# One table for the order and the engines of an attention and gated-MLP kernel on one core

## Chip, core and metric

The kernel runs on 1 core of one Trainium2 chip, in one launch. The metric is the device time of one execution in microseconds (us). The median of three runs of the kernel before is 904.5 us (904.38 to 905.22).

## What is computed

The reference, cut to what matters. `q`, `k` and `v` are 4 x 8 x 768 x 64 (batch, head, position, dimension) in float32, `proj` is 64 x 6, the three weights are 512 x 1536, 512 x 1536 and 1536 x 512:

```python
q_bucket = sum((q @ proj > 0) * 2 ** arange(6))     # hash of each position, the same for k
scores = where(q_bucket[..., :, None] == k_bucket[..., None, :], q @ k.T / 8, -1e9)
attn = exp(scores - max(scores));  attn = attn / (sum(attn) + 1e-09)
x = (attn @ v).transpose(0, 2, 1, 3).reshape(3072, 512)
out = ((x @ w_a) * (x @ w_b)) @ w_out
```

## The kernel before

**Work.** The 3072 tokens are cut into 14 chunks of one or two times 128 tokens (`BLOCKS`). For each chunk the attention output is computed first and then sent through the gated MLP. The last matmuls of a chunk stand in the program between those of the attention of later chunks.

**Attention.** `kprep` and `qprep` (L1127 on) load k and q and call `split` (L709), which scales a tensor by a power of two, writes it as a float16 high part (`kt0`, `qt0`, L648 or L646) and a low part (L748), copies the high part (`hp`, L639), turns both by 128x128 transposes (L766 on PE, with the copy `trk` or `trq` at L639, or by DMA at L757), and adds the hash bits as 12 further rows (L787, L805 to L817). `vprep` (L1031) loads v and makes `vh` and `vl` (L1051). For each tile of 128 queries, `qtile` (L1202) has: scores on PE (L1215), the maximum on DVE (`mx`, L1235), two small steps that give scale and bias (`sc`, `bias`, L1243 and L1247, on DVE or POOL), the exponential on ACT (`e`, L1256). In chunk 0 `turned` (L1181) transposes `e` on PE (`et`, L1191) and copies it back (`at`, L639). In all other chunks `by_dma` (L1163) casts it to a high part `a` (L639, on ACT, DVE or POOL), subtracts that for a low part (L642, on POOL), and turns both by DMA (L1177). Then PE multiplies by v (`av`, L1269 or L1284). After 8 tiles (a chunk of 128 tokens, or half of a larger one) `su_end` (L1292) divides by the sums (`x`, L1335) and turns the result (`px`, `xT`, L1376).

**Weights.** All three weights (18 blocks, two DMAs each) are loaded once, at the start. `to_f32` (L921) loads a block into one of three staging slots (L934, a ring: the fourth block's load waits until the first slot is free) and rebuilds exact float32 values with three steps: a low piece (`third`, L945 on ACT or L947 on POOL), a high piece (L955 on ACT), and both together on DVE (L963), which frees the slot. Every two blocks then get a bound from PE (`slot_gram`, L981, 16 matmuls), DVE (L662) and `power_of` (`w_ai`, L625 and L628).

**MLP.** `moe` (L1389): `ab` on PE (L1442 in float32 for the first two chunks, L1450 with three float16 products for the others), product of both halves on ACT, DVE and POOL (L1471 to L1495), `o` on PE (L1515), `osb` and the store.

**What sets the order.** The functions above only record operations, numbered as they are recorded; each has its engine or the engines allowed, an estimated duration, and what it reads and writes. `Plan.issue` (L400) then replays them with these durations as a list scheduler: whenever an engine is free in the replay, the ready operation with the lowest number in `PLACES` is issued on it (an engine that `ENGINES` names, or the first free one of several). The order in which operations are issued is the order of each engine's instructions, and every engine takes its instructions in that order: one that waits holds back all that stand behind it. The loads and DMA transposes are issued by SP, in its own order. Two recorded operations (`lambda: None`, for `identh` and `identb`) only mark tokens and issue nothing.

Of the kernel before, what the change touches and what calls it, by code (L numbers as in the profile page):

```python
# [61 lines left out]
PLACES = (  # L62
# [234 lines left out]
    3481: "DVE", 3489: "DVE", 3497: "DVE", 3505: "ACT", 3514: "ACT", 3522: "DVE", 3538: "DVE", 3547: "DVE",  # L297
    3568: "ACT", 3576: "ACT", 3584: "ACT", 3592: "DVE", 3601: "ACT", 3634: "DVE", 3635: "DVE", 3725: "DVE",
}

def free(b, **durs):
# [27 lines left out]
HOP = 0.2  # L331
PE_TAIL = 0.2
# [34 lines left out]
class Plan:  # L367
# [32 lines left out]
    def issue(self):  # L400
        ops = self.ops
        for o, place in zip(ops, PLACES):
            o.key = place
            o.eng = ENGINES.get(o.seq, o.eng)
# [1214 lines left out]
```

## Time and profile before

| | us |
|---|---|
| median of three runs | 904.5 |
| lowest and highest run | 904.38, 905.22 |
| span of the profiled execution, first to last instruction | 900.4 |
| busy: PE, DVE, ACT, POOL | 871.8, 624.4, 573.4, 450.9 |

The profile gives the profiled execution by its span; a time of its own, measured as the runs are, is not shown, so 904.5 - 900.4 = 4.1 us are taken as what lies around the span. Lines (L963) are those of the kernel before. A busy time on PE runs from a matmul's start to its modelled end and the matmuls overlap, so that the length of a short row holds some 0.1 to 0.2 us of the row behind it; on DVE and ACT a step's end overlaps the next start by about 0.1 us.

### The profile page before, as it was taken

What the parts mean: (1) busy time and instruction counts of PE and PEld (TensorE: products, weight loads), DVE (VectorE), ACT (ScalarE), POOL (GpSimd) and SP (SyncE); (2) the same over time, 40 slices, a digit from 0 to 9 for tenths busy, and PEclk for the clock granted to TensorE, in tenths of its full rate; (3) what the DMA queues carried; (4) which work ended last, traced back from release to release, by engine and by line L of the source; (5) the groups of instructions that cost most, each with busy time, mean ns of one, the idle gap of its engine ahead of it and who ended that gap; (6) DMA issues with size and microseconds to landing.
All of it is one profiled execution on the core that took longest, in us unless ns stands there. A gap on an engine that the chain in (4) does not pass through costs nothing.

```text
span 900.4 us, 24310 instructions
## 1 busy us (share of the span) xinstructions
PE 871.8 (97%) x9761; PEld 673.8 (75%) x9761; DVE 624.4 (69%) x1446; ACT 573.4 (64%) x1125; POOL 450.9 (50%) x377
## 2 busy tenths in 40 slices
PE   5798999999999999999999999999999999999998
PEld 4677788786877777777777777777777777777775
DVE  6889878897778666777776686777778576633211
ACT  5986565677776878666766675667676466654222
POOL 1255456555735665554455556635556457544111
PEclk9699999999999999999999999999999999999999
DMA  9898667599998999998976788698986757755100
GB/s 331 262 319 232 124 112 158 124 179 220 190 230 148 170 163 161 177 209 169 176 161 128 149 175 169 115 214 170 179 183 148 124 136 130 147 95 100 32 24 24
DMA packets 430433, 145.31 MB, mean 161 GB/s; under 512 B 404080, under 2 KB 422640, under 8 KB 430320
## 3 DMA queue, kind: packets, MB, share of 16 engines
q1 hardware_dynamic: 430160, 143.76, 76.8%
q8 instruction: 76, 1.25, 0.6%
q14 instruction: 37, 0.30, 0.1%
q10 hardware_dynamic: 160, 0.00, 0.0%
HBM read 37.82 MB, written 6.29 MB: 49 GB/s over the span
## 4 chain that ended last, share of the span: by engine, by line
PE 85%; DVE 9%; DMA 2%; issue 2%; ACT 1%; POOL 0%; SPq 0%; DVEq 0%; ACTq 0%; POOLq 0%
PE ab L1450 37%; PE o L1515 20%; PE s L1215 12%; PE av L1284 10%; PE ab L1442 4%; DVE mx L1235 2%; DVE wz L963 1%; PE kt L766 1%; DMA wz<-in_moe_w_out_dram 1%; DVE wz L906 1%; DMA wz<-in_moe_w_b_dram 1%; DMA wz<-in_moe_w_a_dram 1%; DMA pj<-in_proj_dram 0%; PE qb L787 0%; DVE g L1479 0%
## 5 line engine op out<-in xcount | busy, mean ns | idle before, releaser
L642 POOL TENSOR_TENSOR a<-e,a 128x768 f16<-128x768 f32 x184 | 309.4, 1686 | 199.3 <-DVE a L639 87.9
L1450 PE MATMUL ab<-xT,wz 128*128 128x256 f16 (+1 forms) x3456 | 377.5, 264 | 1.4 <-DVE g L1479 1.0
L1450 PEld LDWEIGHTS <-wz 128*128 128x128 f16 x3456 | 310.9, 98 | 52.5 <-issue 3.5
L1256 ACT ACTIVATE e<-s,bias,sc 128x768 f32<-128x768 f32 x192 | 189.8, 989 | 107.4 <-DVE bias L1247 84.5
L1235 DVE TENSOR_REDUCE mx<-s 128x1 f32<-128x768 f32 x192 | 182.7, 953 | 64.1 <-PE s L1215 59.0
L1515 PE MATMUL o<-wz,g 128*128 128x512 f16 (+1 forms) x840 | 215.6, 392 | 0.1
L1495 POOL TENSOR_TENSOR g<-g,g 128x256 f16<-128x256 f32 x132 | 95.8, 726 | 170.8 <-ACT g L1490 164.3
L1215 PE MATMUL s<-trk,trq 76*128 76x384 f16 (+1 forms) x768 | 157.6, 330 | 3.8 <-ACT e L1256 2.5
L1479 DVE SCALAR_TENSOR_TENSOR g<-ab,ab,a 128x256 f32<-128x256 f32 x132 | 63.4, 480 | 105.6 <-ACT a L1471 88.0
L1284 PEld LDWEIGHTS <-at 128*128 128x128 f16 x3312 | 116.9, 98 | 16.2 <-issue 1.7
L1515 PEld LDWEIGHTS <-g 128*128 128x128 f16 x792 | 73.8, 98 | 68.8
L1471 ACT ACTIVATE a<-ab,ab 128x256 f32<-128x256 f32 x132 | 62.2, 471 | 96.2 <-PE ab L1450 79.8
L1284 PE MATMUL av<-vh,at 128*128 128x64 f16 x2208 | 121.6, 193 | 0.7 <-DMA at<-a 0.7
L1215 PEld LDWEIGHTS <-trq 76*128 76x128 f16 (+1 forms) x768 | 70.7, 99 | 45.7 <-issue 9.5
L639 ACT CAST a<-e 128x768 f16<-128x768 f32 x105 | 87.0, 829 | 3.4 <-DMA at<-a 1.4
L1490 ACT CAST g<-g 128x256 f16<-128x256 f32 x132 | 53.0, 401 | 51.3 <-DVE g L1479 41.1
L1284 PE MATMUL av<-vl,at 128*128 128x64 f16 x1104 | 62.3, 193 | 0.0
L639 DVE CAST a<-e 128x768 f16<-128x768 f32 x71 | 42.2, 596 | 14.6 <-ACT e L1256 13.7
L1442 PE MATMUL ab<-xT,wz 128*128 128x128 f32 x384 | 48.1, 278 | 1.3 <-DVE xT L639 0.8
L1442 PEld LDWEIGHTS ab<-xT,wz 128*128 128x128 f32 x384 | 45.5, 192 | 4.6 <-DVE xT L639 1.5
L1247 DVE TENSOR_SCALAR bias<-mx,sc 128x1 f32<-128x1 f32 x180 | 38.6, 214 | 6.3
L1243 DVE TENSOR_SCALAR sc<-mx,cq 128x1 f32<-128x1 f32 x180 | 38.1, 212 | 4.8
(170 smaller groups left out, 775.4 us busy)
## 6 DMA issues: line engine op xcount, KB each, us to landing
rk<-in_k_dram SPq DMA_DIRECT2D x16, 384.0 KB, 4.2
rq<-in_q_dram SPq DMA_DIRECT2D x24, 256.0 KB, 3.5
wz<-in_moe_w_a_dram SPq DMA_DIRECT2D x12, 512.0 KB, 5.7
wz<-in_moe_w_b_dram SPq DMA_DIRECT2D x12, 512.0 KB, 5.3
wz<-in_moe_w_out_dram SPq DMA_DIRECT2D x12, 512.0 KB, 5.7
out_dram<-osb SPq DMA_DIRECT2D x24, 256.0 KB, 2.5
vr<-in_v_dram SPq DMA_DIRECT2D x12, 384.0 KB, 4.7
at<-a SPq DMA_TRANSPOSE x184, 3.5
```

Source lines behind the costliest of these rows:

```text
L639: {"ACT": nc.scalar.copy, "DVE": nc.vector.tensor_copy, "POOL": nc.gpsimd.tensor_copy}[e](out=out, in_=x)
L642: (nc.gpsimd if e == "POOL" else nc.vector).tensor_tensor(out=out, in0=x, in1=y, op=ALU.subtract)
L1215: nc.tensor.matmul(ps.t[:, jj, :HALF], lhsT=trq.t[rows, i, (2 * j + h) * nt + t], rhs=tr.t[rows, i, k0 : k0 + NT // 2].rearrange("p n s -> ...
L1235: lambda: nc.vector.tensor_reduce(out=mx.t[:, col], in_=halves(ps.t), axis=AX.XY, op=ALU.max, negate=True),
L1256: lambda: nc.scalar.activation(flat2(e.t), halves(ps.t), AF.Exp, bias=bias.t[:, col], scale=sc.t[:, col], accum_out=sm.t[:, u : u + 1],),
L1284: nc.tensor.matmul(av.t[:, u, :], lhsT=at.t[:, a + kt, :], rhs=w.t[:, h, kt, :], start=i == 0, stop=i == 3 * NT - 1,)
L1442: nc.tensor.matmul(pl.t[:, m, to], lhsT=wt32(m, cc, f), rhs=xt.t[:, cc * nt // NC, cc * nt % NC : cc * nt % NC + nt, :], start=cc == 0, st ...
L1450: nc.tensor.matmul(pl.t[:, m, to], lhsT=wt(m, wi, cc, f), rhs=xt.t[:, cc * nt // NC, xi, cc * nt % NC : cc * nt % NC + nt, :], start=i == ...
L1471: lambda a=a, pl=pl, gr=gr, sc_of=sc_of: nc.scalar.activation(a.t, pl.t[:, 0, :CH], AF.Copy, scale=sc_of(gr)),
L1479: lambda a=a, g32=g32, pl=pl, gr=gr, sc_of=sc_of: nc.vector.scalar_tensor_tensor(out=g32.t, in0=pl.t[:, 1, :CH], scalar=sc_of(gr + 1), in1 ...
L1495: lambda g=g, g32=g32, g_of=g_of: nc.gpsimd.tensor_tensor(out=g_of(g[1]), in0=g32.t, in1=g_of(g[0]), op=ALU.subtract),
L1515: nc.tensor.matmul(po[u].t.rearrange("p a b -> p (a b)"), lhsT=x()[:, us], rhs=w, start=f == 0 and i == 0, stop=f == NF - 1 and i == len(t ...
```

## The change

`PLACES`, `ENGINES` and the list scheduler go. `ORDER` gives the numbers of all operations in the order in which they are issued, and `ENGINE_OF` one engine for each operation that may run on several. `issue` walks through the list and checks that predecessors are issued and that buffers do not run out. The two operations that issue nothing are dropped and their tokens go to the operations that write the constants, so numbers shift by one or two. What every operation does is as before.

```diff
-PLACES = (
-    372, 36, 26, 591, 571, 25, 386, 254, 1614, 66, 385, 210, 155, 399, 576, 261, 194, 687, 615, 294, 3076, 750, 536,
...
-ENGINES = {
-    17: "DVE", 20: "ACT", 27: "ACT", 33: "DVE", 36: "DVE", 43: "ACT", 49: "DVE", 52: "DVE", 53: "ACT DVE",
...
+ORDER = (
+    9, 10, 75, 76, 4, 77, 11, 2, 0, 3, 78, 79, 80, 84, 12, 13, 14, 27, 28, 1, 5, 81, 15, 16, 82, 29, 281, 83, 6, 282,
...
+ENGINE_OF = {
+    "ACT": (
+        19, 26, 42, 51, 58, 67, 74, 80, 83, 84, 90, 105, 107, 109, 111, 121, 130, 138, 140, 147, 149, 157, 159, 166, 168,
...
     def issue(self):
-        ops = self.ops
-        for o, place in zip(ops, PLACES):
-            o.key = place
-            o.eng = ENGINES.get(o.seq, o.eng)
...
+        engine = {n: e for e, ns in ENGINE_OF.items() for n in ns}
+        issued, live = set(), {}
+        for n in ORDER:
+            o = self.ops[n]
+            assert o.preds <= issued, n
+            issued.add(n)
...
+            if isinstance(o.dur, dict):
+                o.fn(engine[n])
+            else:
+                o.fn()
...
-    op("DVE", 0.2, lambda: None, -85, r=["csb"], w=["identh"])
...
-        op("DVE", 0.2, lambda: None, key, r=["csb"], w=["identb"])
```

The order of PE's operations differs from the old one up to the 384th of 1056, which ran at 284.1 us in the trace before, and is the same behind it; on the other engines the last difference lies between 281 and 285 us too. Of the operations that may run on several engines, 127 get another one, all of them in that stretch. By kind: 9 low pieces of weight blocks go from ACT to POOL (one comes back); 17 pairs of `sc` and `bias` go from DVE to POOL and 6 the other way; 16 casts of `e` go from ACT or DVE to POOL and 3 from POOL to ACT; 14 subtractions for the low part of `e` go from POOL to DVE; 15 high parts and copies of them in `split` go from ACT to DVE and two the other way; 5 copies `at` of chunk 0 go from ACT to DVE and 3 the other way.

**DVE, the last instructions ahead of the first `x` (chunk 0's attention output).** In the names `wz` is the weight store, `po_t` and `ai` are powers of two, `mx_1_0` is the row maximum of chunk 1. Before:

```order
L639 COPY at_0_0_2_1_0_961<-et_0_0_2_1_0_0_969 128x384
L662 TENSOR_REDUCE wost_776<-gram_wo1_978 128x1
L662 TENSOR_REDUCE st_q2_0_1017<-gram_q2_0_997 128x1
L639 CAST a2_1_0_0_0_0_1019<-e_1_0_0_0_0_973 128x768
L963 SCALAR_TENSOR_TENSOR wz_70<-wz_70 128x1024
L625 TENSOR_SCALAR po_t_q2_0_1034<-ps_q2_0_1024 128x1
L628 SCALAR_TENSOR_TENSOR ai_q2_0_1035<-pw_74,po_t_q2_0_1034 128x2
L1226 TENSOR_SCALAR cq_2_0_1044<-ai_q2_0_1035,ai_k0_2_382 128x1
L1226 TENSOR_SCALAR cq_2_0_1044<-ai_q2_0_1035,ai_k0_0_148 128x1
L1226 TENSOR_SCALAR cq_2_0_1044<-ai_q2_0_1035,ai_k0_3_431 128x1
L1235 TENSOR_REDUCE mx_1_0_910<-s_1_0_2_1_0_1027 128x1
L1335 TENSOR_TENSOR x_0_0_1058<-av_0_0_615,r_0_0_930 128x512
```

Now, from five rows ahead of it to five rows behind it:

```order
L1156 TENSOR_REDUCE mx_1_0_886<-s_1_0_0_1_0_869 128x1
L583 TENSOR_REDUCE st_q4_1_899<-gram_q4_1_890 128x1
L884 SCALAR_TENSOR_TENSOR wz_70<-wz_70 128x1024
L1156 TENSOR_REDUCE mx_1_0_886<-s_1_0_0_0_0_914 128x1
L1246 RECIPROCAL r_0_0_852<-r_0_0_852 128x8
L1256 TENSOR_TENSOR x_0_0_929<-av_0_0_641,r_0_0_852 128x512
L546 TENSOR_SCALAR po_t_w0_934<-ps_w0_932 128x1
L549 SCALAR_TENSOR_TENSOR w_ai0_935<-pw_74,po_t_w0_934 128x2
L583 TENSOR_REDUCE wst_463<-gram_w2_944 128x1
L884 SCALAR_TENSOR_TENSOR wz_70<-wz_70 128x1024
L1156 TENSOR_REDUCE mx_1_0_886<-s_1_0_3_1_0_969 128x1
```

Of the 14 weight blocks whose last step (L963, now L884) stood ahead of `x_0_0`, five now stand behind it. So do three of the four `vl`, the four `w_ai` and three bounds. In all, 30 operations that stood ahead of `x_0_0` on DVE are behind it or on another engine, and 14 are new ahead of it: five copies `at`, three pairs of `sc` and `bias`, two high parts and two copies of them, the low part of one q, and one bound of q.

**POOL, its first instructions behind the constants.** L947 (now L868) is the low piece of a weight block; `hp` is the copy of a high part. Before:

```order
L639 COPY hp1_77<-qt0_0_0_193 128x8x64
L639 COPY hp0_76<-kt0_0_1_252 128x12x64
L947 ISA
L947 TENSOR_SCALAR wz_70<-wz_70 128x1024
L1243 TENSOR_SCALAR sc_0_0_480<-mx_0_0_424,cq_0_0_189 128x1
L1247 TENSOR_SCALAR bias_0_0_482<-mx_0_0_424,sc_0_0_480 128x1
L639 COPY hp0_76<-kt0_0_3_473 128x12x64
L947 TENSOR_SCALAR wz_70<-wz_70 128x1024
L1243 TENSOR_SCALAR sc_0_0_480<-mx_0_0_424,cq_0_0_189 128x1
```

Now:

```order
L868 ISA
L868 TENSOR_SCALAR wz_70<-wz_70 128x1024
L560 COPY hp1_77<-kt0_0_0_143 128x12x64
L868 TENSOR_SCALAR wz_70<-wz_70 128x1024
L560 COPY hp0_76<-kt0_0_1_171 128x12x64
L1164 TENSOR_SCALAR sc_0_0_365<-mx_0_0_363,cq_0_0_306 128x1
L1168 TENSOR_SCALAR bias_0_0_367<-mx_0_0_363,sc_0_0_365 128x1
L868 TENSOR_SCALAR wz_70<-wz_70 128x1024 x2
L560 COPY hp0_76<-kt0_0_3_402 128x12x64
L868 TENSOR_SCALAR wz_70<-wz_70 128x1024 x2
```

Of the first nine weight blocks, seven low pieces that ACT had are on POOL now, mixed with the copies and the small steps; the copy for `kt0_0_0` stands behind the first of them.

**SP, the first loads.** Before:

```order
L1017 DMA rk_0_0_93<-in_k_dram 128x2x384
L1144 DMA rq_0_0_95<-in_q_dram 128x8x64
L576 DMA ident_64<-in_cst_dram 128x128
L1017 DMA rk_0_1_100<-in_k_dram 128x2x384
L1065 DMA v0_2_102<-in_v_dram 128x2x384
L1065 DMA v0_0_110<-in_v_dram 128x2x384
L1065 DMA v0_3_126<-in_v_dram 128x2x384
L934 DMA wz_70<-in_moe_w_a_dram 128x1024
L1065 DMA v0_1_134<-in_v_dram 128x2x384
L934 DMA wz_70<-in_moe_w_a_dram 128x1024
```

Now, the first rows and those that follow them:

```order
L1065 DMA rq_0_0_84<-in_q_dram 128x8x64
L938 DMA rk_0_0_99<-in_k_dram 128x2x384
L498 DMA ident_64<-in_cst_dram 128x128
L938 DMA rk_0_1_126<-in_k_dram 128x2x384
L855 DMA wz_70<-in_moe_w_a_dram 128x1024 x2
L938 DMA rk_0_2_178<-in_k_dram 128x2x384
L855 DMA wz_70<-in_moe_w_a_dram 128x1024 x2
L938 DMA rk_0_3_219<-in_k_dram 128x2x384
L855 DMA wz_70<-in_moe_w_b_dram 128x1024 x2
L986 DMA v0_1_300<-in_v_dram 128x2x384
L986 DMA v0_3_303<-in_v_dram 128x2x384
L1065 DMA rq_1_0_326<-in_q_dram 128x8x64
```

```order
L855 DMA wz_70<-in_moe_w_b_dram 128x1024 x2
L986 DMA v0_2_370<-in_v_dram 128x2x384
L855 DMA wz_70<-in_moe_w_out_dram 128x1024 x2
L986 DMA v0_0_554<-in_v_dram 128x2x384
L855 DMA wz_70<-in_moe_w_out_dram 128x1024 x2
```

The q of the first chunk is loaded first, the four v (`v0_0` to `v0_3`) stand behind three, three, four and five weight blocks (in the order `v0_1`, `v0_3`, `v0_2`, `v0_0`), where they stood among the first nine loads; `v0_0` is behind the fifth block's loads, whose staging slot has to be freed first.

On PE, the first `ab` stands behind 80 operations instead of 85. Three of the seven `slot_gram` that stood ahead of it are behind it now, with three `power_of`, and one bound of a q (L675, four matmuls) is new ahead of it.

## Rows read from the trace of the kernel before

**Rows 1.** The page, its head and part 1 (busy time, share of the span, instructions).

```profile
span 900.4 us, 24310 instructions
...
PE 871.8 (97%) x9761; PEld 673.8 (75%) x9761; DVE 624.4 (69%) x1446; ACT 573.4 (64%) x1125; POOL 450.9 (50%) x377
```

**Rows 2.** Busy time by engine in five stretches (start:end, length, busy us and count).

```profile
0.00:76.50 76.50, 56.60 (x568) 47.96 (x568) 63.24 (x149) 60.33 (x86) 25.41 (x32) 0.87 0.93 293
76.50:100.00 23.50, 22.91 (x225) 19.40 (x226) 22.19 (x36) 15.71 (x25) 9.24 (x7) 1.00 0.67 182
100.00:200.00 100.00, 99.01 (x1212) 79.53 (x1211) 84.48 (x183) 63.52 (x116) 57.16 (x43) 1.00 0.71 145
200.00:300.00 100.00, 98.07 (x1268) 75.80 (x1267) 74.89 (x189) 72.70 (x152) 60.20 (x51) 1.00 0.99 194
300.00:900.40 600.40, 595.21 (x6494) 451.14 (x6492) 379.59 (x892) 361.17 (x750) 298.89 (x248) 1.00 0.74 141
```

**Rows 3.** Timeline of PE: start, length, line, output, what idle time ended on.

```profile
6.01 0.16 PE L613 MATMUL ps_pj<-st_pj,onesr 128*128 128x1 bf16 x1 [6.01 <-ACT pjx L653]
...
76.51 5.62 PE L1442 MATMUL ab<-xT,wz 128*128 128x128 f32 x48 [0.81 <-DVE xT L639]
82.25 1.08 PE L981 MATMUL gram_w<-wz 128*128 128x128 bf16 x16
```

**Rows 4.** Timeline of DVE before the first normalised output x.

```profile
66.47 1.82 DVE L963 SCALAR_TENSOR_TENSOR wz<-wz 128x1024 int32<-128x1024 int32 x1
...
69.72 1.23 DVE L963 SCALAR_TENSOR_TENSOR wz<-wz 128x1024 int32<-128x1024 int32 x1
...
73.74 0.68 DVE L1335 TENSOR_TENSOR x<-av,r 128x512 f32<-128x512 f32 x1
```

**Rows 5.** DVE groups by line and shape, 0 to 77 us (count, busy us, mean ns).

```profile
L963 DVE SCALAR_TENSOR_TENSOR wz<-wz 128x1024 int32<-128x1024 int32 x14 | 17.6, 1265 | 2.7 <-ACT wz L945 1.4 <-POOL wz L947 1.2
L1235 DVE TENSOR_REDUCE mx<-s 128x1 f32<-128x768 f32 x12 | 11.4, 948 | 2.2 <-PE s L1215 1.3 <-PE ps_k L613 0.8
...
L1051 DVE SCALAR_TENSOR_TENSOR vl<-v,v_ai,vh 128x768 f16<-128x768 f32 x4 | 4.1, 1013 | 0.0
L639 DVE COPY trk<-kt 128x1536 f16<-128x1536 f16 x3 | 2.8, 948 | 0.0
L1226 DVE TENSOR_SCALAR cq<-ai_q,ai_k 128x1 f32<-128x1 f32 x11 | 2.0, 208 | 0.1
...
L628 DVE SCALAR_TENSOR_TENSOR w_ai<-pw,po_t_w 128x2 int32<-128x2 f32 x4 | 1.6, 396 | 0.1
L639 DVE COPY at<-et 128x384 f32<-128x384 f32 x3 | 1.6, 543 | 0.0
...
L748 DVE SCALAR_TENSOR_TENSOR qt<-rq,ai_q,qt 128x512 f16<-128x512 f32 x2 | 1.9, 965 | 0.1
...
L648 DVE TENSOR_SCALAR vh<-v,v_ai 128x768 f16<-128x768 f32 x2 | 1.1, 610 | 0.0
...
L639 DVE CAST a<-e 128x768 f16<-128x768 f32 x1 | 0.5, 547 | 0.0
```

**Rows 6.** Chain that ended last, three pieces around 40 to 49 us (start, length).

```profile
40.76 4.70 DMA wz<-in_moe_w_a_dram
...
45.67 1.16 ACT wz L955
...
48.69 4.85 DMA wz<-in_moe_w_b_dram
```

**Rows 7.** POOL groups by line and shape, 0 to 77 us.

```profile
L947 POOL TENSOR_SCALAR wz<-wz 128x1024 int32<-128x1024 uint8 x7 | 8.9, 1267 | 22.8 <-DVE wst L662 9.0 <-DMA wz<-in_moe_w_b_dram 5.5 <-DMA wz<-in_moe_w_out_dram 2.2
```

**Rows 8.** Timeline of POOL around those two steps of DVE.

```profile
66.11 1.12 POOL L947 TENSOR_SCALAR wz<-wz 128x1024 int32<-128x1024 uint8 x1 [0.29 <-DMA wz<-in_moe_w_a_dram]
69.77 4.29 POOL L642 TENSOR_TENSOR a<-e,a 128x768 f16<-128x768 f32 x2 [2.54 <-DVE a L639]
```

**Rows 9.** POOL groups by line and shape, 76.5 to 300 us.

```profile
L642 POOL TENSOR_TENSOR a<-e,a 128x768 f16<-128x768 f32 x54 | 93.4, 1736 | 62.4 <-DVE a L639 36.1 <-ACT a L639 17.8 <-issue 2.9
```

More of the change, by code (lines that the diff above doesn't have):

```diff
@@ L1 @@
-import heapq
 from contextlib import ExitStack
@@ L299 @@
+ORDER = (
[187 rows of a table added]
+)
+ENGINE_OF = {
+    "ACT": (
[11 rows of a table added]
+    ),
+    "DVE": (
[17 rows of a table added]
+    ),
+    "POOL": (
[13 rows of a table added]
+    ),
 }
@@ L350, in __init__ @@
         self.shape, self.dtype, self.name = shape, dtype, name
-        self.real, self.left, self.free_at = None, 0, 0.0
+        self.real, self.left, self.held = None, 0, False
     @property
@@ L400, in issue @@
     def issue(self):
-        ops = self.ops
-        for o, place in zip(ops, PLACES):
-            o.key = place
-            o.eng = ENGINES.get(o.seq, o.eng)
-        for o in ops:
-            o.succs, o.npred, o.ready = [], len(o.preds), 0.0
-        for o in ops:
-            for p in o.preds:
-                ops[p].succs.append(o)
-        free = {e: 0.0 for e in ("PE", "ACT", "DVE", "POOL", "SP")}
-        ready = {e: [] for e in free}
-        for o in ops:
-            if not o.npred:
-                for e in o.eng.split():
-                    ready[e].append(o)
@@ L501, in issue @@
-        return now
+        engine = {n: e for e, ns in ENGINE_OF.items() for n in ns}
[4 more added lines that the diff above has]
+            issued.add(n)
+            for b in o.bufs:
+                if not b.held:
+                    b.held = True
+                    for k, limit in b.limits:
+                        live[k] = live.get(k, 0) + 1
+                        assert live[k] <= limit, (n, k)
+            if isinstance(o.dur, dict):
+                o.fn(engine[n])
+            else:
+                o.fn()
+            for b in o.bufs:
+                b.left -= 1
+                if not b.left:
+                    for k, _ in b.limits:
+                        live[k] -= 1
+                    if b.ring is not None:
+                        b.ring.append(b.real)
@@ L504, in attention_moe @@
+        assert len(issued) == len(self.ops)
 @with_exitstack
@@ L740, in high @@
                 nc.vector.tensor_copy(out=identh, in_=ident)
+        first = ["identh"] * (x == "0_0" and which == "k")
         op(
             "ACT DVE", {"ACT": 0.3 + 0.83e-3 * size, "DVE": 0.24 + 0.54e-3 * size},
-            high, key, r=[*toks, ai], w=[(pt[0], "hi")], sbuf=True,
+            high, key, r=[*toks, ai] + ["csb"] * len(first), w=[(pt[0], "hi"), *first], sbuf=True,
         )
@@ L865, in both @@
                 )
-        op("DVE", 0.2, both, key, r=[*((wst, g) for g in range(NG)), wo_ai], w=[wm], sbuf=True)
+        op("DVE", 0.2, both, key, r=["csb", *((wst, g) for g in range(NG)), wo_ai], w=[wm, "identb"], sbuf=True)
         ps = psum("ps_bounds", tag)
```

122 lines of the change are left out of this document (removed), and 417 rows, old and new, of tables (ENGINE_OF, ORDER, PLACES).

## Prediction

> **What bounds the kernel now.** I read the page's busy times first, then the same by stretch, then what PE waited for in the one stretch where it waits. PE is busy 871.8 of 900.4 us [rows 1]. By stretch [rows 2] the rest is uneven: behind 300 us PE is busy 595.21 of 600.40 us, and from 100 to 300 us 2.9 us are missing; in the first 76.5 us 19.9 are, and the mean granted clock there (the column behind the counts) is 0.87, which is 1.00 everywhere else. So the kernel is PE's own work, with a start in which PE waits. The timeline of PE shows the two ends of that start [rows 3]: the first matmul waits until 6.01 us for the projection, and the first `ab` of the MLP stands at 76.51 us, behind a copy on DVE. In between DVE is the full engine: busy 63.24 of the 76.5 us [rows 2], though it gets nothing from PE before 6.01 us, so nine tenths of the rest. From 76.5 us on PE has MLP matmuls to put between the steps of attention, and waits for little.
>
> The order is the same behind 285 us, where PE is full. The forecast is therefore a sum over the first 285 us, and what is won or lost there shifts the end by as much.
>
> **The change part by part.** The step that counts is `x_0_0`, at 73.74 us [rows 4]: the MLP cannot start before it.
>
> *DVE ahead of it.* Thirty operations leave. By the means of their groups [rows 5]: five weight blocks' last steps, 5 x 1.265 = 6.3; three `vl`, 3 x 1.013 = 3.0; two copies `trk`, 2 x 0.948 = 1.9; one `mx`, 0.95; three `at`, 3 x 0.543 = 1.6; two `vh`, 2 x 0.610 = 1.2; one cast of `e`, 0.55; four `w_ai`, 4 x 0.396, each with a short step ahead of it that I put at the 0.2 of a `cq`, 2.4; three `cq`, three bounds and three pairs of `sc` and `bias`, twelve instructions at the same 0.2, 2.5. Together 20.4 us. Fourteen come in: five `at`, 2.7; the low part of a q, 0.97; two high parts like `vh`, 1.2; two copies of them at no more than 0.54, 1.1; three pairs of `sc` and `bias` and a bound, 1.4. Together 7.4. That is 13.0 us less, and 16 entries fewer, whose overlaps with their neighbours (a little under 0.1 us each) no clock would show: 12.0. The bounds: nothing is gained if what paces DVE is not its own work but the ring of weight loads, which stands in the chain [rows 6] as a load of 4.70 us, a step of ACT, and the next load 7.9 us later (40.76 to 48.69). But that ring is shortened as well: 9 blocks instead of 14 stand ahead of `x_0_0`, three rounds of three slots instead of five, up to 2 x 7.9 us off the chain. I stay at 12.0, since a DVE that is nine tenths full is the nearest row; the lower end is 0.
>
> *ACT* hands seven low pieces to POOL and several copies to DVE and gets two `trk`; with 60.33 of 76.5 us busy before [rows 2] it doesn't become the bound. *POOL* was busy 25.41; seven low pieces at 1.267 [rows 7] are 8.9 us more, which fit.
>
> *PE ahead of the first `ab`.* Three `slot_gram` at 1.08 us [rows 3] are put off and one of a quarter of the size comes in: PE has 3.0 us more left to do when it starts on the MLP: -3.0.
>
> *What was put off.* Five block steps, three `vl`, four `w_ai` and the bounds, some 12 us of DVE work, now fall into the time that was freed, while PE has matmuls to do. DVE is busy 22.19 of the 23.5 us behind 76.5 us and 84.48 of the next 100 [rows 2], so something will be late: the `ab` of later columns need the blocks. I take 1.5 us back; the ends are 0 and 12, all of it.
>
> *From 100 to 285 us.* The 2.9 us that PE waits there [rows 2] are the most that a better order can give; I take half, +1.5. What is moved there (casts to POOL, 14 subtractions from POOL to DVE) lies beside PE's work.
>
> *Queues.* On SP the loads of v stand behind up to five weight blocks. The fifth block's load waits for a staging slot, and `v0_0` behind it; no matmul needs it before chunk 0's first `av`, well behind the first scores. I cost that at nothing, covered by the steps of the first tile; if the slot is freed late, `v0_0` is what is late next. PE's first matmul no longer waits for the projection but for q, which is loaded first: at most some of the 6.01 us, and not counted. The two dropped entries issue nothing: 0.
>
> Sum: 12.0 - 3.0 - 1.5 + 1.5 = 9.0 us. The profiled execution's span would be 900.4 - 9.0 = 891.4 us; with the 4.1 us that the median of the runs shown lies above it, **895.5 us**.
>
> **A rule that speaks against it.** A block step of DVE that started at 66.47 us, while POOL was on a low piece of 66.11 to 67.23, took 1.82 us; the one of 69.72, just ahead of POOL's next step, took 1.23 [rows 4, 8]. The Trainium skill, "SBUF — State Buffer", section "Who interferes with whom", has a rule for it: a DVE instruction with two SBUF inputs and a GpSimd instruction that reads SBUF share one interface, and the one that issues second is fully blocked until the first is done. By that rule each low piece moved to POOL can hold DVE for as long as POOL runs, and most of the 12.0 us would be lost. The rows bear out the blocking; what it cost there was 0.6 us, since DVE came when half of POOL's step was over.
>
> **The rivals.**
>
> *POOL takes back what DVE saves.* Seven low pieces are new on POOL ahead of `x_0_0`, where DVE is full. At 0.6 us each [rows 4] 4.2 us are lost: 899.7 us; at their whole length, 8.9 us [rows 7], 904.4. For it: the two rows above. Against: POOL did seven low pieces in this stretch already, and DVE's mean for the block step, 1.265, is hardly above the 1.23 of one alone. Chance 0.14.
>
> *The work put off comes back.* If all of the 12 us reach PE as waits for weight blocks between 65 and 110 us, nothing is left of the gain: 904.5 us. Against it: nine blocks are ready by then, and PE has chunk 0's matmuls to do while the others follow. Chance 0.07.
>
> *Slower: DVE becomes the bound between 100 and 285 us.* Its place is the low part of `e`. Fourteen subtractions go from POOL to DVE, where each has two SBUF inputs against a POOL that still does the others, at 1.736 us each [rows 9], and gets the casts. One that has to wait for POOL holds all that is behind it on DVE, the maxima above all, for up to 1.7 us, and PE waits at its next scores or `av`. It decides when more than 9.0 / 1.74, five, of the 14 show in full; with eight, 13.9 us, the time is 895.5 + 13.9 = 909.4 us, with all 14, 24.3 us, 919.8. For it: 41 us of DVE's 200 are idle between 100 and 300 us [rows 2], not much with 12 us put off into it. Against: 17 pairs of `sc` and `bias` leave DVE in return for six, and PE waited only 2.9 us there. Chance 0.09.
>
> *More than forecast.* If the work put off costs nothing and PE's waits up to 285 us go, the gain is 12.0 - 3.0 + 2.9 = 11.9: 892.6 us. The earlier start adds to that, and a granted clock of 0.87 over 76.5 us is 10 us of lost clock [rows 2], mostly under PE's waits: should PE wait less and the clock hold, the matmuls in the chain get shorter: 888 with half of that. Chance 0.10 for below 890.
>
> **How the numbers follow.** The forecast of 895.5 us, with 890 to 899 around it, has a chance of 0.60. The range from 888 to 902.5 us takes in the forecast, most of POOL's rival and most of the case of more; outside lie the hidden gain, the slower case and the ends of the others, together 2 in 10. About 0.2%, 1.8 us, can be told from no change. Faster: 0.60 + 0.10 + 0.13 of POOL's 0.14 = 0.83; within 0.2%: 0.07 + 0.01 = 0.08; slower: 0.09.
>
> **What would show it.** Right: `x` of chunk 0 at about 62 us instead of 73.74 and the first `ab` at about 65; PE's idle time up to the first `ab` well below 19.9 us; the same busy time of PE behind 285 us, all shifted by some 9 us. POOL's rival: block steps of DVE with a mean well above 1.265 ahead of `x`. The hidden gain: `x` early, and gaps on PE behind a block step between 65 and 110 us. The slower case: gaps on PE behind `mx`, `bias` or `at` from 100 to 285 us, and subtractions on DVE that wait. The forecast is wrong if `x` comes no earlier than 70 us, or if the first `ab` is 9 us early and PE has lost it again by 285 us.

## The result and the profile after

The change is slower: 908.88 us (median of 4 runs, 908.25 to 909.84) against 904.44 (4 runs on the same chip, 903.17 to 905.22), a ratio of 1.0054 with a 95% interval of 1.004 to 1.0068. Forecast were 895.5 us, within 888.0 to 902.5. The profiled execution has a span of 906.9 us, against 900.4.

The page of the changed kernel, busy times, answers to [rows 1]. PE's own work is the same; ACT has 18 us less than before, DVE 17 more, POOL 20 more:

```profile
PE 871.7 (96%) x9761; PEld 674.7 (74%) x9761; DVE 641.3 (71%) x1440; ACT 555.2 (61%) x1102; POOL 471.4 (52%) x406
```

The same by stretch, for [rows 2] (columns: stretch, length, busy time and count for PE, PEld, DVE, ACT and POOL, the granted clock, DMA share, GB/s):

```profile
0.00:76.50 76.50, 59.04 (x624) 52.77 (x624) 63.27 (x148) 50.25 (x77) 33.67 (x39) 0.98 0.85 269
76.50:100.00 23.50, 20.16 (x166) 15.18 (x167) 18.65 (x41) 14.51 (x23) 17.69 (x15) 0.93 0.87 226
100.00:200.00 100.00, 93.46 (x1111) 74.50 (x1109) 91.48 (x161) 62.94 (x111) 70.68 (x59) 0.98 0.82 153
200.00:300.00 100.00, 97.60 (x1322) 77.16 (x1319) 84.27 (x193) 61.89 (x135) 45.41 (x46) 1.00 0.96 181
300.00:906.90 606.90, 601.45 (x6547) 455.04 (x6544) 383.58 (x901) 365.65 (x759) 303.96 (x251) 1.00 0.75 142
```

Up to 76.5 us PE is busy 59.04 us instead of 56.60, and its mean granted clock is 0.98 instead of 0.87. Behind that it idles more than before: 3.3 us instead of 0.6 from 76.5 to 100, 6.5 instead of 1.0 from 100 to 200, 2.4 instead of 1.9 from 200 to 300. Behind 300 us nothing has changed (5.5 us idle, before 5.2). POOL, busy 57.16 of 100 us from 100 to 200 before, is now busy 70.68; DVE 91.48 instead of 84.48.

Where the lead goes is read from `x`, the attention output of each chunk, in the timeline of DVE. The kernel before (its first `x`, at 73.74, is in [rows 4]):

```profile
120.77 0.68 DVE L1335 TENSOR_TENSOR x<-av,r 128x512 f32<-128x512 f32 x1
...
152.80 0.69 DVE L1335 TENSOR_TENSOR x<-av,r 128x512 f32<-128x512 f32 x1 [0.57 <-PE av L1284]
...
188.37 0.68 DVE L1335 TENSOR_TENSOR x<-av,r 128x512 f32<-128x512 f32 x1
...
215.24 0.68 DVE L1335 TENSOR_TENSOR x<-av,r 128x512 f32<-128x512 f32 x1
```

After (L1256 is L1335 of before):

```profile
60.02 0.69 DVE L1256 TENSOR_TENSOR x<-av,r 128x512 f32<-128x512 f32 x1
...
119.70 0.68 DVE L1256 TENSOR_TENSOR x<-av,r 128x512 f32<-128x512 f32 x1
...
146.87 0.69 DVE L1256 TENSOR_TENSOR x<-av,r 128x512 f32<-128x512 f32 x1
...
183.83 0.67 DVE L1256 TENSOR_TENSOR x<-av,r 128x512 f32<-128x512 f32 x1
...
219.13 0.69 DVE L1256 TENSOR_TENSOR x<-av,r 128x512 f32<-128x512 f32 x1
```

The first `x` comes 13.7 us early, where 12.0 were forecast. The second is early by 1.1 us only, the third by 5.9, the fourth by 4.5, the fifth 3.9 us late. The timeline of PE after has the first `ab` and the waits behind it (in brackets the idle time ahead and what ended it):

```profile
64.60 2.77 PE L1363 MATMUL ab<-xT,wz 128*128 128x128 f32 x12
...
83.65 0.81 PE L1136 MATMUL s<-trk,trq 76*128 76x384 f16 x4 [1.41 <-DVE po_t_q L546]
...
93.33 0.81 PE L1136 MATMUL s<-trk,trq 76*128 76x384 f16 x4 [1.77 <-ACT e L1177]
...
190.28 0.55 PE L1436 MATMUL o<-wz,g 128*128 128x512 f16 x1 [3.19 <-POOL g L1416]
...
204.87 1.50 PE L1371 MATMUL ab<-xT,wz 128*128 128x128 f16 x24 [1.28 <-DVE g L1400]
```

The first `ab` stands at 64.60 us, 11.9 us ahead of before [rows 3]. To follow the lead I take from the time of a matmul the usual lengths of all PE steps issued ahead of it; what is left is the time that PE has lost by then, an estimate from the traces that is good to about 1 us. At the first `ab` it is 34.4 us before and 25.1 after: **9.3 us won**. At 100 us it is 36.2 and 33.7, at 170 us 38.5 and 37.0, at 210 us 39.5 and **47.2**, at 290 us 42.2 and 48.3; from there on both grow alike. So the lead melts to 2.5 us by 100 us, and 10.2 us are lost between 170 and 210 us where the kernel before lost 1.0. That loss is what there is to explain.

It has a conspicuous spot. POOL's timeline there (L1164 and L1168 are `sc` and `bias`, L563 the subtraction for the low part of `e`, L1416 the last product of the MLP's `g`):

```profile
177.89 4.33 POOL L563 TENSOR_TENSOR a<-e,a 128x768 f16<-128x768 f32 x2 [1.25 <-ACT a L560]
184.01 0.30 POOL L1164 TENSOR_SCALAR sc<-mx,cq 128x1 f32<-128x1 f32 x1 [1.79 <-DVE mx L1156]
...
185.86 2.37 POOL L1164 TENSOR_SCALAR sc<-mx,cq 128x1 f32<-128x1 f32 x1 [1.19 <-DVE mx L1156]
188.33 1.15 POOL L1168 TENSOR_SCALAR bias<-mx,sc 128x1 f32<-128x1 f32 x1
189.56 0.67 POOL L1416 TENSOR_TENSOR g<-g,g 128x256 f16<-128x256 f32 x1
```

and DVE's (L569 and L560: high part of a q and its copy; L827: the last step of a halving, which turns two float32 slots of a weight into float16 parts for the chunks behind the first two):

```profile
178.85 1.87 DVE L569 TENSOR_SCALAR qt<-rq,ai_q 128x512 f16<-128x512 f32 x1
180.76 1.62 DVE L560 COPY hp<-qt 128x512 f16<-128x512 f16 x1
...
185.68 3.66 DVE L827 SCALAR_TENSOR_TENSOR wz<-wz,w_ai 128x1024 f16<-128x1024 f32 x3
```

The `sc` at 184.01 us took 0.30 us; that at 185.86, of the same shape, took 2.37 beside DVE's three weight steps of 185.68 to 189.34, and its `bias` 1.15. DVE's high part took 1.87 us and its copy 1.62, beside two subtractions of POOL that end at 182.22 us; the copy ends at 182.38. `g` stands behind that pair in POOL's queue, and PE's `o` waits 3.19 us for it. The windows of this spot show what follows the wait: PE busy 1.52 of 6.30 us, then a granted clock of 0.52 and 0.55, its lower level of 1.2 GHz, for 3.7 us:

```profile
184.00:190.30 6.30, 1.52 (x25) 0.79 (x23) 5.38 (x7) 3.54 (x7) 4.82 (x6) 1.00 1.07 180
190.30:192.10 1.80, 1.80 (x21) 1.56 (x22) 1.21 (x3) 1.53 (x5) 1.72 (x2) 0.52 0.48 107
192.10:194.00 1.90, 1.90 (x33) 1.90 (x31) 1.90 (x3) 0.51 (x2) 1.90 (x3) 0.55 0.00 0
```

### The profile page after: what moved, and what is told of

Its sections match the earlier page's. It is cut to its first block, busy times and chain, and to the rows that moved or that the text cites. A ratio compares the mean times of both kernels' runs of the same rounds, so it can differ in the third digit from the quotient of the medians.

```text
span 906.9 us, 24285 instructions
## 1 busy us (share of the span) xinstructions
PE 871.7 (96%) x9761; PEld 674.7 (74%) x9761; DVE 641.3 (71%) x1440; ACT 555.2 (61%) x1102; POOL 471.4 (52%) x406
## 4 chain that ended last, share of the span: by engine, by line
PE 77%; DVE 13%; POOL 3%; ACT 3%; issue 3%; DMA 1%; SPq 0%; DVEq 0%; ACTq 0%; POOLq 0%
PE ab L1371 35%; PE o L1436 18%; PE s L1136 11%; PE av L1205 9%; DVE mx L1156 3%; DVE wz L884 1%; ACT e L1177 1%; PE ab L1363 1%; DVE wz L827 1%; DMA wz<-in_moe_w_a_dram 1%; DVE g L1400 1%; POOL a L563 1%; POOL a L560 1%; POOL sc L1164 1%; POOL bias L1168 1%
## 5 line engine op out<-in xcount | busy, mean ns | idle before, releaser
L563 POOL TENSOR_TENSOR a<-e,a 128x768 f16<-128x768 f32 x170 | 289.7, 1709 | 150.2 <-ACT a L560 57.3
L1416 POOL TENSOR_TENSOR g<-g,g 128x256 f16<-128x256 f32 x132 | 96.5, 731 | 188.2 <-ACT g L1411 183.1
L1136 PE MATMUL s<-trk,trq 76*128 76x384 f16 (+1 forms) x768 | 154.7, 325 | 7.5 <-ACT e L1177 4.9
L1136 PEld LDWEIGHTS <-trq 76*128 76x128 f16 (+1 forms) x768 | 70.3, 98 | 49.0 <-issue 12.4
L560 ACT CAST a<-e 128x768 f16<-128x768 f32 x99 | 82.0, 829 | 4.7 <-POOL a L563 1.5
L1363 PEld LDWEIGHTS ab<-xT,wz 128*128 128x128 f32 x384 | 48.7, 200 | 5.3 <-issue 3.1
L1363 PE MATMUL ab<-xT,wz 128*128 128x128 f32 x384 | 51.6, 286 | 0.7 <-DVE wst L583 0.7
L560 DVE CAST a<-e 128x768 f16<-128x768 f32 x64 | 38.2, 597 | 15.8 <-ACT e L1177 15.3
L1168 DVE TENSOR_SCALAR bias<-mx,sc 128x1 f32<-128x1 f32 x169 | 36.2, 214 | 5.9
L1164 DVE TENSOR_SCALAR sc<-mx,cq 128x1 f32<-128x1 f32 x169 | 35.7, 211 | 4.4
```

Of the source, the lines that this page charges most:

```text
L560: {"ACT": nc.scalar.copy, "DVE": nc.vector.tensor_copy, "POOL": nc.gpsimd.tensor_copy}[e](out=out, in_=x)
L563: (nc.gpsimd if e == "POOL" else nc.vector).tensor_tensor(out=out, in0=x, in1=y, op=ALU.subtract)
L1136: nc.tensor.matmul(ps.t[:, jj, :HALF], lhsT=trq.t[rows, i, (2 * j + h) * nt + t], rhs=tr.t[rows, i, k0 : k0 + NT // 2].rearrange("p n s -> ...
L1363: nc.tensor.matmul(pl.t[:, m, to], lhsT=wt32(m, cc, f), rhs=xt.t[:, cc * nt // NC, cc * nt % NC : cc * nt % NC + nt, :], start=cc == 0, st ...
L1416: lambda g=g, g32=g32, g_of=g_of: nc.gpsimd.tensor_tensor(out=g_of(g[1]), in0=g32.t, in1=g_of(g[0]), op=ALU.subtract),
```

## The experiments

All kernels below are compared with the kernel before on the same chip; ratios are to it, with a 95% interval, and the change itself stands at 1.0054. "Change" is the changed kernel, numbers are those of `ORDER`, `BEFORE` is the order of the kernel before in these numbers; where that kernel itself is edited, it is written as such a table. Long lists of numbers are written short in the diffs, and an operation that is put on one engine is taken off the other. The lettered theories are explained where they first occur; F stands for two of them, one at the seams and another at the conspicuous spot.

**One kind of move put back.** Three kernels keep the order and put one class of operations back on its old engine, behind 100 us; a fourth goes over to the old order and engines at 172 us.

```diff
 ENGINE_OF = {
     "DVE": (
...
+        610, 618, 737, 746, 865, 873, 898, 906, 960, 985, 993, 1001,
```

> The change with 12 pairs sc/bias, which it moved from DVE to POOL behind 100 us, put back on DVE; order as changed. In the changed kernel PE loses 9.9 us between 172 and 215 us (time less PE work rises from 37.3 to 47.2), and there POOL's six sc take 1011 ns in the mean where one alone takes 0.3, the longest 2.37 us beside three weight steps of DVE. Theory A (the pairs on POOL are blocked there and hold g and the exponentials behind them): most of the 9 us come back, 900 to 903 us against 908.9. Theory B (POOL has too much work of any kind there, casts above all): 2 to 4 us, 905 to 907. Theory C (the prediction's slower rival: subtractions on DVE): no change, 908 to 910, or later still, as DVE gets 12 pairs more. Theory D (the order of 172 to 215 us itself): no change.

Measured: 912.26 us, 1.0088 (1.0075 to 1.0101). Slower than the change: A is out as the whole cause.

```diff
 ENGINE_OF = {
     "ACT": (
...
+        595, 714, 756, 900, 908, 916, 924, 954, 962,
...
     "DVE": (
...
+        578, 731,
```

> The change with 11 casts of e, which it moved to POOL behind 100 us, put back (9 on ACT, 2 on DVE). Theory A: little, 907 to 909. Theory B (POOL is overfull between 172 and 215 us): POOL has 5 casts of 0.82 to 1.8 us less there, most of the loss goes, 900 to 904. Theories C and D: 908 to 910.

Measured: 912.08 us, 1.0086 (1.0072 to 1.0101). Slower too, and slower than any of the theories had it: taking the casts off POOL does not bring the loss back.

```diff
 ENGINE_OF = {
...
     "POOL": (
...
+        587, 740, 774, 917, 963, 971, 979, 988, 1012, 1184, 1200, 1208, 1241, 1297,
```

> The change with the 14 subtractions that it moved from POOL to DVE put back on POOL. Theory C (the slower rival of the prediction, these subtractions on DVE): the loss goes, 899 to 903. Theories A and B: POOL gets 2 subtractions more between 172 and 215 us and 9 behind, so the same or slower, 909 to 915. Theory D: 908 to 910.

Measured: 911.57 us, 1.008 (1.0067 to 1.0092). So the prediction's slower rival did not name the right place: with the 14 subtractions back on POOL the kernel is 2.4 us slower by the ratios, not faster.

```diff
+ORDER = ORDER[:764] + tuple(n for n in BEFORE if n not in ORDER[:764])
```

> Order and engines of the change for its first 764 operations (up to 172 us), and what is left in the order and on the engines of the kernel before. At this seam PE has lost 37.3 us in the change and 38.6 before. If the loss lies in what is done behind the seam (A, B, C or D, all of them): 904.4 less 1.3 us, 902.5 to 904. If it was made ahead of the seam, by work put off to behind it, it shows again: 907 to 910.

Measured: 910.13 us, 1.0063 (1.005 to 1.0076). With the old order behind 172 us PE loses as much: 39.0 us at 180 us, 47.4 at 200. Either the loss was made ahead of the seam, or the seam makes one of its own.

**Earlier seams, and less work on DVE.** Two kernels change over at 52 and at 86 us. Two more make the last step of six halvings cheaper, in the change and as a control in the kernel before.

```diff
+ORDER = ORDER[:240] + tuple(n for n in BEFORE if n not in ORDER[:240])
```

> Order and engines of the change for its first 240 operations (up to 52 us), the rest as in the kernel before. There PE has lost 22.8 us in the change and some 28.5 before. Theory E (debt: what the change puts off, weight blocks and their halvings on DVE, is owed and falls due between 172 and 215 us): by 52 us hardly a block has been put off, so most of the 5.7 us stay, 899 to 901. Theory F (the lead of PE is only borrowed, since the vector engines set when the later tiles of attention are done): it melts whatever the seam, 903.5 to 905.

Measured: 910.58 us, 1.0083 (1.0066 to 1.0099). Neither theory: the lead of 5.7 us was lost within 30 us. The old order wants weight blocks at once that the new one has put off (PE's bounds wait 6.8 us for them between 50 and 90 us); the window behind the seam has PE busy 18.27 of 26.50 us at a granted clock of 0.66:

```profile
50.00:76.50 26.50, 18.27 (x129) 15.26 (x128) 22.18 (x40) 15.26 (x23) 11.07 (x11) 0.66 0.88 305
```

```diff
+ORDER = ORDER[:390] + tuple(n for n in BEFORE if n not in ORDER[:390])
```

> The same with the seam behind 390 operations (86 us), where PE has lost 29.5 us in the change and 35.0 before, but where the change is several weight blocks and five halvings behind. Theory E: the debt falls due, 905 to 910. Theory F: 903.5 to 905. If only what stands behind 86 us cost time: 904.4 less 5.5, 899.

Measured: 913.87 us, 1.0115 (1.0097 to 1.0134). The same at a later seam, with more put off: PE has lost 29.5 us ahead of it and 49.0 at 120 us. So the seams show that work had been put off, but they make waits of their own, perhaps that of 172 us too, and don't tell where the change loses its time.

```diff
+COPIED = (6, 8, 10, 18, 20, 22)
...
-            lambda: nc.vector.scalar_tensor_tensor(
+            lambda: nc.vector.tensor_copy(out=lo(), in_=hi()) if to in COPIED else nc.vector.scalar_tensor_tensor(
```

> The change, with the last step of six halvings (those that end on DVE between 185 and 203 us, 1.27 to 1.84 us each, two inputs from SBUF) replaced by a copy of the high half in 16 bits; the low half of these weights is so left out of the result. Theory E: DVE owes 5 us less and holds POOL less just where the loss lies, 901 to 905. If DVE's weight steps are not what PE waits for there: 908 to 909.

Measured: 904.42 us, 1.002 (1.0008 to 1.0032): by the ratios 3.1 us faster than the change.

> The same six steps replaced in the kernel before, as a control: PE hardly waits there, so 903.5 to 904.6 in either theory; well below that would mean that these steps cost time in both orders and tell nothing of the change.

Measured: 904.14 us, 1.0001 (0.9989 to 1.0013). So these six steps, which DVE runs between 185 and 203 us in the change and between 146 and 200 us in the kernel before, are on PE's path in the one and not in the other. Whether by their own length or by how long they hold POOL, the two runs do not tell.

**Order, engines, and the first rival.**

```diff
-        engine = {n: e for e, ns in ENGINE_OF.items() for n in ns}
+        engine = {n: e for e, ns in ENGINES_BEFORE.items() for n in ns}
```

> The order of the change with every operation on the engine it had before (127 put back). Theory G (the change takes 22 us of work from ACT, up to 285 us, and gives it to POOL and DVE, which block each other: the time that DVE's steps take beyond their length alone grows from 15 to 30 us up to 215 us): without the new engines at most 904.4, 899 to 904. Theory E (the order owes weight steps that fall due between 172 and 215 us): the loss stays or grows, as the order was made for the other engines, 908 to 915.

Measured: 938.54 us, 1.0382 (1.0366 to 1.0398). The other half, the old order with the new engines:

```diff
-        for n in ORDER:
+        for n in BEFORE:
```

> The order of before with the engines of the change. Theory G: 908 to 915. Theory E: 903 to 906.

Measured: 932.43 us, 1.0302 (1.0288 to 1.0316). Far outside every expectation: either half costs some 30 us, both together 5. Order and engines fit each other and cannot be costed one by one; with that, what putting a whole class back costs, above and below, says little about the class.

```diff
 ENGINE_OF = {
     "ACT": (
...
+        283, 288, 302, 311, 323, 328, 337, 377, 391,
```

> The change with the nine low pieces of weight blocks, which it moved from ACT to POOL ahead of 105 us, put back on ACT. The prediction's first rival (low pieces on POOL block DVE's block steps ahead of the first x): x and all behind it earlier, 901 to 906. Theory E: the front has its gain already and the debt stays, 908 to 911. Theory G: POOL has 9 to 11 us less there, 905 to 908.

Measured: 912.3 us, 1.0084 (1.007 to 1.0097). Slower than any theory had it. The first `x` stands at 66.06 us in this run and at 60.02 in the change, so that the low pieces on POOL did not take back what DVE had saved ahead of it, which was the first rival.

Putting back all 52 operations that had left ACT:

```diff
         engine = {n: e for e, ns in ENGINE_OF.items() for n in ns}
+        engine.update((n, "ACT") for n in LEFT_ACT)
```

> The change with all 52 operations that left ACT for DVE or POOL put back on ACT, order as changed. ACT idles 17 of 35 us between 180 and 215 us, where POOL is busy 25.4. Theory G: most of the loss goes, 899 to 905. Theory E: 907 to 913, since DVE keeps the owed steps and ACT's queue gets 50 steps more at places that were made for others.

Measured: 931.15 us, 1.0285 (1.0261 to 1.0309). Expected by neither; like the two halves above it mostly measures a list made for other engines.

**The conspicuous spot taken apart.**

```diff
     "DVE": (
...
+        898,
```

> The change with a single pair, the sc/bias that stands at 185.86 us on POOL, put back on DVE. Theory H (one meeting of this pair with three weight steps of DVE holds POOL's g and so PE, and the wait costs the clock): the wait of 3.19 us at 190.28 and the slow clock behind it go, 3 to 6 us, 903 to 906. Theory F (DVE and POOL together are full up to 215 us, whichever has what): PE waits elsewhere, 907.5 to 909.5.

Measured: 909.81 us, 1.0055 (1.0036 to 1.0074): no gain. The wait did shrink, from 3.19 to 0.94 us, but the timeline of PE shows others in its place, on a q's DMA and on DVE:

```profile
188.08 0.39 PE L1437 MATMUL o<-wz,g 128*128 128x512 f16 x1 [0.94 <-POOL g L1417]
...
196.74 0.82 PE L1137 MATMUL s<-trk,trq 76*128 76x384 f16 x4 [1.38 <-DMA trq<-hp]
...
204.62 1.50 PE L1372 MATMUL ab<-xT,wz 128*128 128x128 f16 x24 [2.25 <-DVE g L1401]
```

```diff
 ORDER = (
...
-    529, 527, 648,
+    648, 529, 527,
```

> The change with two of the three weight steps moved on DVE behind the next g, the pair still on POOL. Theory H: POOL's pair is held by one step instead of three, 1.3 us instead of 3.5, and g of DVE comes early: 903 to 906 as well. Theory F: 907.5 to 909.5.

Measured: 909.26 us, 1.0063 (1.0045 to 1.0081).

```diff
 ORDER = (
...
-    941, 905,
+    905, 941,
...
-    916, 925, 660,
+    660, 916, 925,
...
     "ACT": (
...
+        940, 943,
```

> Both of these, and two more meetings taken apart: two high parts of a q (1.87 and 1.62 us on DVE beside POOL's subtractions at 178.85 and 180.76) on ACT, which idles there, with mx ahead of the low part; and a cast and a subtraction of POOL behind the g at 202.64 that waits for them. Theory H: most of the 9 us, 900 to 903, below the kernel before. Theory F: 906 to 909.

Measured: 907.65 us, 1.0043 (1.0027 to 1.0059): some 1 us less than the change, within both intervals. Theory H falls: neither that meeting nor all those taken apart here cost the 9 us.

**POOL's subtractions made to read nothing.** What was left to try was the sum of all meetings.

```diff
+ZEROED = ("1_", "2_", "3_", "4_0_")
...
-            lambda eng: minus(eng, a2.t[:, S:], e.t, a2.t[:, :S]), key, r=[e, (a2, 0)], w=[(a2, 1)], sbuf=True,
+            lambda eng: nc.gpsimd.memset(a2.t[:, S:], 0.0) if eng == "POOL" and n.startswith(ZEROED)
+            else minus(eng, a2.t[:, S:], e.t, a2.t[:, :S]), key, r=[e, (a2, 0)], w=[(a2, 1)], sbuf=True,
```

> The change with 28 subtractions of POOL (tiles 1 to 4, the first half of tile 4) replaced by a fill with zeros on POOL, which reads nothing; the low part of these e is so left out of the result. DVE's and ACT's work are untouched. Theory G (POOL's overlap lengthens DVE's steps, and DVE is the bound up to 210 us): DVE's steps get shorter by 5 us or more ahead of 215 us and the time falls by as much or more, to 898 to 904. Theory E (DVE's own list in this order is what is late): 906 to 909.

Measured: **894.87 us, 0.9908** (0.9889 to 0.9926), 13.2 us faster than the change by the ratios, and more than theory G had expected. The first `ab` stands at 65.11 us, no earlier than in the change (64.60), so all of this is won behind it. The windows of the change:

```profile
100.00:170.00 70.00, 68.84 (x760) 55.52 (x758) 65.23 (x125) 42.92 (x75) 45.92 (x39) 1.00 0.84 162
170.00:215.00 45.00, 37.71 (x583) 30.33 (x582) 38.30 (x62) 26.83 (x52) 33.46 (x30) 0.96 0.83 143
```

and of this run, in which PE no longer waits between 100 and 170 us, and idles 3.8 us from 76.5 to 215 us where it idled 11.8 in the change:

```profile
76.50:100.00 23.50, 22.34 (x213) 16.72 (x211) 22.69 (x47) 18.09 (x28) 13.24 (x17) 1.00 1.09 271
100.00:170.00 70.00, 70.00 (x816) 57.39 (x815) 60.80 (x130) 46.03 (x82) 29.46 (x43) 1.00 0.86 166
170.00:215.00 45.00, 42.37 (x667) 34.19 (x665) 38.08 (x71) 30.55 (x63) 27.19 (x33) 1.00 0.91 174
```

The same pair still meets the same three weight steps, with the same lengths (POOL's timeline of this run), so this meeting was not what cost the time:

```profile
174.95 2.37 POOL L1169 TENSOR_SCALAR sc<-mx,cq 128x1 f32<-128x1 f32 x1 [1.20 <-DVE mx L1161]
177.41 1.15 POOL L1173 TENSOR_SCALAR bias<-mx,sc 128x1 f32<-128x1 f32 x1
```

The control is the same edit in the kernel before, where 32 subtractions of these tiles are on POOL (in the change four of them are on DVE):

> The same 32 subtractions of POOL replaced in the kernel before, as a control: PE waits for little there, so 902 to 904.5 in either theory.

Measured: 899.31 us, 0.9958 (0.994 to 0.9976), 3.8 us faster than before, below the range expected. The ten runs lie between 896.60 and 903.13 us, and the profiled one took 901.97, with a span of 900.1 us; it doesn't show where the 3.8 us come from. So with these subtractions out of the way the change is faster than the kernel before with the same edit, 0.9908 / 0.9958 = 0.995, some 4.5 us; with them it is 4.9 us slower. What differs is what they cost: 13.2 us in one order, 3.8 in the other.

What became shorter is shown by DVE's groups from 75 to 215 us, those with the largest differences. The change (line, engine, operation, shapes, count | busy us, mean ns):

```profile
L827 DVE SCALAR_TENSOR_TENSOR wz<-wz,w_ai 128x1024 f16<-128x1024 f32 x12 | 16.5, 1390 | 0.0
...
L827 DVE SCALAR_TENSOR_TENSOR wz<-wz,wo_ai 128x1024 f16<-128x1024 f32 x6 | 9.1, 1514 | 0.1
...
L739 DVE TENSOR_SCALAR hp<-bits_q 128x48 f16<-128x48 f32 x5 | 3.7, 746 | 0.0
...
L736 DVE TENSOR_SCALAR hp<-bits_q 128x48 f16<-128x48 f32 x5 | 3.6, 714 | 0.1
...
L569 DVE TENSOR_SCALAR qt<-rq,ai_q 128x512 f16<-128x512 f32 x4 | 3.3, 825 | 0.0
...
L560 DVE COPY hp<-qt 128x512 f16<-128x512 f16 x3 | 2.2, 729 | 0.0
```

The same groups without the subtractions (lines are four further down):

```profile
L831 DVE SCALAR_TENSOR_TENSOR wz<-wz,w_ai 128x1024 f16<-128x1024 f32 x12 | 15.2, 1277 | 0.0
...
L831 DVE SCALAR_TENSOR_TENSOR wz<-wz,wo_ai 128x1024 f16<-128x1024 f32 x6 | 8.3, 1378 | 0.9 <-ACT wz L571 0.9
...
L740 DVE TENSOR_SCALAR hp<-bits_q 128x48 f16<-128x48 f32 x5 | 2.1, 411 | 0.1
L573 DVE TENSOR_SCALAR qt<-rq,ai_q 128x512 f16<-128x512 f32 x4 | 1.9, 478 | 0.0
...
L743 DVE TENSOR_SCALAR hp<-bits_q 128x48 f16<-128x48 f32 x5 | 1.0, 199 | 0.0
...
L564 DVE COPY hp<-qt 128x512 f16<-128x512 f16 x3 | 0.9, 288 | 0.0
```

The same work takes 1.3 us less in the first group, 0.8 in the second, 2.7 and 1.5 in the two of the hash bits, 1.4 in the high parts of q and 1.3 in their copies, of DVE operations that the edit did not touch. A copy of a high part takes 288 ns with POOL filling zeros and 729 with POOL subtracting. Other groups moved both ways, some by as much (casts of `e` from 552 to 876 ns). DVE has the same instructions in the same order in both runs, so they can be compared one by one: from 75 to 285 us they are 12.4 us shorter in all, 6.3 of it between 170 and 215 us.

The kernel before had such meetings too. Two of its groups in the same stretch, with the subtractions:

```profile
L906 DVE SCALAR_TENSOR_TENSOR wz<-wz,w_ai 128x1024 f16<-128x1024 f32 x12 | 16.7, 1400 | 0.1
...
L648 DVE TENSOR_SCALAR wz<-wz,w_ai 128x1024 f16<-128x1024 f32 x3 | 5.0, 1651 | 0.0
```

and without them:

```profile
L832 DVE SCALAR_TENSOR_TENSOR wz<-wz,w_ai 128x1024 f16<-128x1024 f32 x12 | 15.3, 1278 | 0.1
...
L574 DVE TENSOR_SCALAR wz<-wz,w_ai 128x1024 f16<-128x1024 f32 x3 | 2.2, 747 | 0.0
```

Compared one by one, its DVE instructions from 75 to 285 us are 9.5 us shorter without the subtractions, 1.7 of it between 170 and 215 us. So POOL's subtractions held DVE for nearly as long in the old order as in the new. What the new order altered is where they do it, and that PE waits for it.

POOL's own time for the replaced operations falls as well, in the change from 27 x 1.92 to 27 x 0.76 us between 75 and 215 us. The run does not tell how much of the 13.2 us came by DVE's shorter steps and how much by POOL's shorter queue, in which `sc` and `g` wait.

```diff
+COPIED = (36, 38, 40, 42, 44, 46)
```

> The change with the last step of six other halvings, on DVE between 114 and 168 us, replaced by a copy as in the run with six copies (the low half of these weights is left out of the result). If DVE is full from 100 us up to 210 us: the 4.5 us of that run again, 903.5 to 906. If only DVE's work behind 180 us is on the path: 908 to 909.

Measured: 907.86 us, 1.0047 (1.003 to 1.0064), 0.6 us less than the change and no difference that can be told. Some 0.85 us less DVE work in each of six steps there does not reach PE. Together with the run with zeros, for which it gave 906 to 909, this speaks against theory E, a debt that DVE carries along from 100 us on.

## Why the prediction was wrong

*DVE ahead of the first `x`, 12.0 us, and PE's work put off, 3.0:* right. DVE is busy 48.73 us ahead of the first `x`, where it was busy 60.52: 11.8 us less. The other 1.9 of the 13.7 us are idle time of DVE at the start, where PE's first matmul waits until 3.93 us instead of 6.01; the prediction had not counted that. The first `ab` came 11.9 us early with 2.6 us less PE work done, 9.3 us in place of 9.0. DVE's block steps had a mean of 1.229 us up to 60 us, below the 1.265 of [rows 5]. The low pieces did hold other steps: the low part of a k took 1.73 us twice (13.90 and 26.68 us) and 1.01 once, and a copy of a high part at 29.67 us took 1.26, each of the slow ones beside a low piece on POOL. Against 1.01 and the 0.35 us that such a copy takes later, these are some 2.3 us, which the 11.8 hold already.

*What was put off, 1.5 us back:* mis-sized. 6.8 of the 9.3 us were gone by 100 us (the lead was 2.5 us then), with waits of 1.41 and 1.77 us on DVE and ACT and a granted clock of 0.93 from 76.5 to 100 us. It was not the work put off alone: in the run with zeros, which puts off the same work, PE idles 1.2 us of that stretch instead of 3.3, at a granted clock of 1.00.

*From 100 to 285 us, +1.5, since what is moved there "lies beside PE's work":* **the step that failed**. PE lost 8.6 us more than before there: 14.6 us from 100 to 290 us (33.7 to 48.3) against 6.0 (36.2 to 42.2). In the new order DVE's and POOL's work there lies on PE's path: six shorter steps on DVE gave 3.1 us, and nothing in the old order, and POOL's subtractions replaced gave 13.2 us, against 3.8. I weighed the stretch by the 2.9 us that PE waited in the old order, and by busy times one engine at a time. POOL looked free, at 57 of 100 us, and I costed the steps that it was given at their length alone, and what POOL and DVE do to each other at nothing. It went to 71. That the two hold each other was not new, 9.5 us of DVE's time in the old order and 12.4 in the new; new is that PE waits for it. That the run without POOL's subtractions came out at 894.87 us, near the 895.5 that I had forecast, does not make the sum right, since the same edit gained 3.8 us before as well.

*The rule:* the section of the Trainium skill that I weighed, "Who interferes with whom" in "SBUF — State Buffer", was read for steps with two inputs only, and applied to seven low pieces only. The rows show one-input steps of DVE held as well: a copy of a high part 1.62 us instead of 0.29. The same section of the Trainium skill says that copies, casts and `tensor_scalar` can take the shared interface too, when their operands meet conditions that it refers to. The Trainium skill also says there that a DVE step with two inputs meets a GpSimd instruction that reads, not one that only writes; the run with zeros agrees, its weight steps have means of 1.277 and 1.378 us against 1.390 and 1.514.

*The rivals:* the slower one gave 909.4 us, and 908.9 was measured, but that is luck: its reason only half held. DVE and POOL did get into each other's way between 100 and 285 us, by the subtractions of `e`; but what cost time is those that POOL kept, and with the 14 that went to DVE put back the kernel was 2.4 us slower. "POOL takes back what DVE saves" had the mechanism and the wrong place. The sign that I had set for a wrong forecast, a first `ab` 9 us early whose lead is lost by 285 us, is what the profile showed.

*Open:* whether DVE's held steps or POOL's queue weighs more in the 13.2 us; why PE waits for both in the new order and hardly in the old; and what takes the part of the lead that is gone ahead of 76.5 us. No kernel that does the whole computation came out below the kernel before.

## What to carry to other kernels

Before moving work to an engine that looks idle, look up what its instructions do to a neighbour that is busy, and whether anyone waits for that neighbour. Here POOL's subtractions lengthened DVE's steps by 9.5 us in the old order and 12.4 in the new; making them a fill was worth 13.2 us in the new order (28 of them) and 3.8 us in the old one (32), and the busy times of the page showed nothing of it. A lead at the start is worth what the following stretches let through, so the next engine to fill must be costed over the whole stretch in which the lead could be lost, at lengths that hold under overlap. A change of order and of engines found together is predicted as one thing: its halves cost 30 us each here, and their sum says nothing of the whole.

## What the runs showed of the hardware

A step of POOL on 128 x 1 values, 0.30 us alone, took 2.37 us beside three weight steps of DVE (3.66 us in all): longer than one of them, so it was held by more than one. A step of DVE on 128 x 48 values, 0.18 to 0.20 us alone, had a mean of 0.75 us in the change, over five; without POOL's subtractions it had 0.20. After PE had been busy 1.52 of 6.30 us its granted clock was 0.52 to 0.55 for 3.7 us, and 1.00 behind them.
